# Moving loads, stores and operand work in the feed-forward part of a fused attention kernel

## The chip, the cores and the metric

The kernel runs on one core of one Trainium2 chip. The metric is the device time of one execution in microseconds (us), as the median of several runs. Engines are named as the profile names them: PE (TensorE matmuls), PEld (its weight loads), DVE (VectorE), ACT (ScalarE), POOL (GpSimd), SP (SyncE, whose queue SPq issues nearly all DMAs of this kernel).

## The reference, cut to what matters

Attention over 4 batches, 8 heads, 768 positions and 64 channels, masked to pairs whose keys and queries fall into the same hash bucket (6 sign bits of a projection), and then a feed-forward layer with a piecewise activation on the 3072 tokens:

```python
mask = q_bucket[:, :, :, None] == k_bucket[:, :, None, :]
scores = np.where(mask, scale * np.matmul(q, k.transpose(0, 1, 3, 2)), -1e9)
attn = np.exp(scores - scores.max(-1, keepdims=True))
attn = attn / (attn.sum(-1, keepdims=True) + 1e-09)
x = np.matmul(attn, v).transpose(0, 2, 1, 3).reshape(3072, 512)
h = x @ w_in                                   # 512 x 2048
g = np.where(h >= 1, h, np.where(h <= -1, 0.0, (h + 1) ** 2 / 4))
out = g @ w_out                                # 2048 x 512
```

## The kernel before, in words

Each fp32 factor of a product is split into a high part (rounded to the matmul's input type, fp32r) and a low part (what is left), and a product is three matmuls: high x high, high x low, low x high.

The first part, attention, runs to about 480 us and is not touched. It leaves for each batch b in DRAM the unnormalised output `xd`, the maxima `ed` and the sums' reciprocals `rd`, and the split first weight matrix in SBUF (`wbig` and parts of the tiles `t`) and DRAM (`wq`).

The second part, `ffn`, works on eight chunks of 384 tokens, chunk c = 2b and 2b + 1 of batch b. The order of its work is written out by hand: lists `prep[n]` and `post[n]` hold what is issued before and after the matmuls of step n. `at` appends to the first list, `after` to the second. Each engine, and the DMA queue of SyncE, works in the order in which the program issues.

- **Direct steps**, n = 0 to 31 (480 to 613 us): batch 0. A step is `gemm1` (L772, 12 matmuls into PSUM bank `h`), the activation (ACT: `t`, `z`, L617 and L618; DVE: L623 and L624), the split of the result (`ghi` on ACT, L628; `glo` on DVE, L632), and nine second-layer matmuls (L657, into `y`) of the unit three steps earlier. Beside these DVE splits the blocks of w_out (L70, L74, L78, L82), each from a load into `wraw` (L62, two buffers).
- **Products**, k = 0 to 167 (from 617 us): batches 1 to 3, 56 products each. First-layer blocks of two hidden tiles are computed with seven products instead of eight (`PRODUCTS`, a scheme of Strassen's kind). A product is six matmuls L867, of which the second bank `h` is free only when the product two before it has been read: on ACT by L873 (s = 0) or on DVE by L875 to L887 (s = 1, 3, 4, 5, 6). Then come 4 to 6 matmuls L657. The product's weights are read from a ring of nine tiles (`w_load`, L830), each loaded again from `wc` in DRAM when the product that used it is done.

Three kinds of side work feed the products.

- `w_plan` builds the four summed weight blocks of a pair of hidden tiles: `w_get` loads two blocks from `wq` into `tmp[:, 0]` (L730, L731), `w_sum` adds on DVE into `sumw`, `w_hi` casts on ACT into `tmp[:, 1]` (L739), `w_lo` subtracts on DVE into `tmp[:, 0]`, `w_put` stores both to `wc` (L746, L747).
- `x_plan` builds the fourteen operand tiles of half a batch (cc = 0 or 1): `x_raw` loads four tiles of `xd` into `pc0` to `pc3` (L675); for each of them `x_er` loads a broadcast row of `ed` into `pc4` and of `rd` into `pc5` (L682, two halves each); `x_norm` combines them on DVE (L686, L688); then sums (L697), high parts on ACT (L700) and low parts on DVE (L39).
- `flush` copies a finished `y` on ACT into a tile `ot` (L646, two buffers) and stores it (L647).

Of the kernel before, what the change touches and what calls it, by code (L numbers as in the profile page):

```python
# [22 lines left out]
P = 128  # L23
# [550 lines left out]
def ffn(ctx, tc, wpair, woh, wol, xm, xa, xb, areas, wst, wq, wc, out, prep, post):  # L574
# [29 lines left out]
    def operand(b, o, cc, t):  # L604
        return sets[(b - 1) % 2][cc * 2 * NBLK + 2 * o + t]

# [29 lines left out]
    def flush(c, m):  # L636
# [8 lines left out]
        ot = xp.tile([P, DM], F32, name="ot", bufs=2)  # L645
# [31 lines left out]
    def x_er(b, cc, k):  # L677
        ct, sl = 2 * (k % 2) + cc, slice(k // 2 * CH, (k // 2 + 1) * CH)
        for t, d in ((pc[4], xm.e_d[b]), (pc[5], xm.r_d[b])):
            for h in range(2):  # L680
                r = 2 * ct + h
                nc.sync.dma_start(out=t[64 * h:64 * h + 64], in_=d[r:r + 1, sl].partition_broadcast(64))  # L682

    def x_norm(b, cc, k):
        ct, sv = 2 * (k % 2) + cc, spc[b % 2]
        nc.vector.scalar_tensor_tensor(out=pc[k], in0=pc[4], scalar=sv[:, ct, 0:1], in1=pc[k],  # L686
                                       op0=ALU.mult, op1=ALU.add)
        nc.vector.tensor_tensor(out=pc[k], in0=pc[k], in1=pc[5], op=ALU.mult)  # L688
# [16 lines left out]
    def x_plan(b, cc, raw, norm, made):  # L705

        at(raw, x_raw, b, cc)
        after(raw, x_er, b, cc, 0)
        for k, n in enumerate(norm):
            at(n, x_norm, b, cc, k)  # L710
            if k < 3:
                after(n, x_er, b, cc, k + 1)
        for o, n in made:
# [35 lines left out]
    def w_plan(i, n):  # L749
        at(n, w_get, i)  # L750
        at(n + 1, w_sum, 0)
        at(n + 2, w_sum, 1)
        at(n + 2, w_sum, 2)
        for t in range(2):
            after(n + 2 + t, w_hi, t)
            at(n + 3 + t, w_lo, t)
        at(n + 4, w_put, i)
# [19 lines left out]
    N1 = 2 * NFT  # L777
# [6 lines left out]
    for i in range(NFT // 2):  # L784
        at(8 + i, w_plain, i)
        w_plan(i, (20, 24, 28)[i] if i < 3 else N1 + 6 * (i - 3))
    x_plan(1, 0, 9, (11, 13, 15, 17), ((0, 18), (1, 18), (3, 19), (2, 19), (4, 20), (5, 21), (6, 21)))
    x_plan(1, 1, 22, (24, 25, 26, 27), ((0, 27), (1, 28), (3, 28), (2, 29), (4, 29), (5, 30), (6, 30)))
    for b in (2, 3):
        t0 = N1 + 56 * (b - 2)  # L790
# [4 lines left out]
    at(N1 + 2, lambda: xm.sums_load(*(t[:, 0:NF] for t in pc[4:6]), B - 1))  # L795
    at(N1 + 6, xm.sums_add)
    at(N1 + 6, xm.sums_inv, B - 1)

# [18 lines left out]
    for u in pend:  # L817
# [3 lines left out]
    ring = [t.rearrange("p a b -> p (a b)").bitcast(F32R)[:, n * DM:(n + 1) * DM]  # L821
            for t in [wst.tile([P, DM, 2], I32, name="wraw") for _ in range(2)] for n in range(2)]
    ring += [tu[:, n * DM:(n + 1) * DM] for n in range(3, 6)] + [wpair[15][:, t] for t in range(2)]
    cm, cu = (wst.tile([P, DM], F32, name="wsq")[:, 0:CH] for _ in range(2))
    cv = wst.tile([P, DM], I32, name="wa", bufs=1).bitcast(F32)[:, 0:CH]
    NK = (B - 1) * (NFT // 2) * NBLK

    def w_load(k):
        if k < NK:
            nc.sync.dma_start(out=ring[k % NRING].bitcast(F32),  # L830
# [261 lines left out]
```

## Time and profile before

| | |
|---|---|
| median of the runs | 1049.91 us (1048.38 to 1053.71, 3 runs) |
| the profiled execution | 1052.17 us, span 1050.4 us, mean granted clock 0.993 |
| PE busy | 984.1 us (94%) |
| DVE busy | 793.7 us (76%) |
| ACT busy | 681.1 us (65%) |
| attention, 0 to 500 us | PE 474.1 busy of 500 |
| direct steps, 488.9 to 620.3 us | PE 126.5 busy of 131.4 |
| products 0 to 27, 620.3 to 707.6 us | PE 70.6 busy of 87.3 |
| products 28 to 55, 707.6 to 774.7 us | PE 63.0 busy of 67.1 |
| products 56 to 111, 774.7 to 912.1 us | PE 129.9 busy of 137.4 |
| 49 products, 912.1 to 1022.2 us | PE 110.1 busy of 110.1 |

The stages are cut at ACT's copy L873, which follows every seventh product. Two things are needed to read the numbers. Consecutive matmuls overlap in the records, so a stage is best judged by the time that a product takes in it, not by PE's busy share. And a wait that the profile puts down to DVE or ACT may begin further back: these engines work in order, and one of their own instructions may be waiting for a DMA, which in its turn waited in SyncE's queue.

### The profile page before, as it was taken

Reading aid. Unit: us, or ns where it says so; the run is one execution under the profiler, and the core shown is the slowest. Engines: PE = TensorE matmul, PEld = TensorE weight load, DVE = VectorE, ACT = ScalarE, POOL = GpSimd, SP = SyncE. Lnnn points to the kernel's source line nnn. Section 1 sums busy time; section 2 is a strip of 40 time slices with the busy share of each in tenths; the row PEclk is TensorE's granted clock in tenths of the full one; section 3 lists DMA queues with packets and bytes.
Section 4 is the critical chain, followed back from the end, with each engine's and each line's share of the span. In section 5 each row is a group of like instructions: output and inputs, shape, how many; then the busy total and the mean of one; then the engine's idle time right before and its main releaser. Section 6 shows DMA issues by size and latency. Waiting matters only on the chain.

```text
span 1050.4 us, 15678 instructions
## 1 busy us (share of the span) xinstructions
PE 984.1 (94%) x5036; PEld 893.3 (85%) x5036; DVE 793.7 (76%) x1356; ACT 681.1 (65%) x1489; POOL 344.3 (33%) x412
## 2 busy tenths in 40 slices
PE   5899999999999999999999969879998999999997
PEld 4789989899999999988989858668787888888885
DVE  7779989899999999886789657666765767555553
ACT  5779888899889889886456444344453545454443
POOL 6667767777778778562000000000000000000000
PEclk9999999999999999999999998999999999999999
DMA  3645657776666665643772467847456474454431
GB/s 96 173 119 138 172 152 183 179 185 169 181 168 175 172 170 146 154 109 113 243 232 81 166 218 234 247 158 216 130 148 201 112 198 112 122 169 121 113 88 61
DMA packets 95449, 166.19 MB, mean 158 GB/s; under 512 B 15112, under 2 KB 52616, under 8 KB 95368
## 3 DMA queue, kind: packets, MB, share of 16 engines
q1 hardware_dynamic: 95152, 165.20, 56.3%
q8 instruction: 40, 0.66, 0.3%
q14 instruction: 41, 0.34, 0.1%
q10 hardware_dynamic: 216, 0.00, 0.0%
HBM read 106.13 MB, written 33.87 MB: 133 GB/s over the span
## 4 chain that ended last, share of the span: by engine, by line
PE 60%; DVE 14%; DMA 12%; ACT 8%; issue 3%; SPq 2%; POOL 0%; DVEq 0%; ACTq 0%
PE y L657 14%; PE h L867 11%; PE smax L258 5%; PE s L298 5%; PE o L332 5%; PE o L330 5%; PE o L331 5%; PE s L297 5%; DMA t<-te 5%; PE h L772 3%; DMA pc<-rd 3%; DVE t L623 2%; ACT t L617 2%; ACT z L618 2%; DVE nm L262 2%
## 5 line engine op out<-in xcount | busy, mean ns | idle before, releaser
L306 ACT ACTIVATE ph<-s 128x384 fp32r<-128x384 f32 x380 | 188.1, 495 | 54.0 <-PE s L298 46.2
L262 DVE TENSOR_REDUCE nm<-smax 128x1 f32<-128x768 f32 x186 | 176.5, 949 | 25.9 <-PE smax L258 24.1
L39 POOL TENSOR_TENSOR pl<-pf,ph 128x384 fp32r<-128x384 f32 x128 | 141.2, 1108 | 84.8 <-ACT pf L311 82.7
L623 DVE SCALAR_TENSOR_TENSOR t<-t 128x384 f32<-128x384 f32 x128 | 71.3, 557 | 108.7 <-ACT z L618 108.6
L39 DVE TENSOR_TENSOR pl<-s,ph 128x384 fp32r<-128x384 f32 x256 | 135.9, 545 | 15.7 <-ACT s L311 13.8
L298 PE MATMUL s<-t 128*128 128x384 f32 x384 | 131.5, 343 | 6.3 <-DMA t<-te 6.2
L297 PE MATMUL s<-t 128*128 128x384 f32 x384 | 132.1, 344 | 0.8 <-DVE t L212 0.8
L332 PE MATMUL o<-pl,va 128*128 128x386 f32 x384 | 130.4, 340 | 0.3 <-DVE pl L39 0.3
L330 PE MATMUL o<-ph,va 128*128 128x386 f32 x384 | 130.2, 339 | 0.0
L331 PE MATMUL o<-ph,vb 128*128 128x386 f32 x384 | 129.6, 337 | 0.0
L657 PE MATMUL y<-t,ghi 128*128 128x512 f32 x384 | 125.1, 397 | 0.6 <-ACT ghi L628 0.6
L311 ACT ACTIVATE s<-s 128x384 f32<-128x384 f32 x252 | 125.3, 497 | 0.0
L258 PE MATMUL smax<-t 128*128 128x384 f32 x372 | 100.7, 351 | 5.3 <-DVE nm L262 4.4
L628 ACT CAST ghi<-z 128x384 fp32r<-128x384 f32 x129 | 65.1, 505 | 47.2 <-DVE z L624 42.0
L867 PE MATMUL h<-wbig,t 128*128 128x384 f32 x399 | 83.6, 342 | 6.3 <-DVE wsq L887 4.0
L617 ACT ACTIVATE t<-wsq,mh 128x384 f32<-128x384 f32 x48 | 29.6, 617 | 90.3 <-DVE wsq L881 56.3
L867 PEld LDWEIGHTS h<-wbig,t 128*128 128x128 f32 x399 | 71.6, 190 | 15.5 <-DVE wsq L887 5.2
L657 PEld LDWEIGHTS y<-t,ghi 128*128 128x128 f32 x384 | 71.8, 189 | 12.0 <-ACT ghi L628 1.1
L618 ACT ACTIVATE z<-t,m 128x384 f32<-128x384 f32 x128 | 79.0, 617 | 4.2
L298 PEld LDWEIGHTS s<-t 128*128 128x128 f32 x384 | 72.4, 189 | 10.9 <-DMA t<-te 10.7
L867 PE MATMUL h<-wbig,wraw 128*128 128x384 f32 x321 | 68.2, 347 | 13.9 <-DVE wsq L875 6.7
L258 PEld LDWEIGHTS smax<-t 128*128 128x128 f32 x372 | 64.3, 188 | 19.4 <-DVE nm L262 18.4
(142 smaller groups left out, 2117.5 us busy)
## 6 DMA issues: line engine op xcount, KB each, us to landing
t<-wc SPq DMA_DIRECT2D x92, 256.0 KB
t<-t SPq DMA_DIRECT2D x60, 384.0 KB
wraw<-wc SPq DMA_DIRECT2D x76, 256.0 KB
raw<-in_qk_dram SPq DMA_DIRECT2D x15, 768.0 KB
wraw<-in_w_in_dram SPq DMA_DIRECT2D x16, 512.0 KB
wraw<-in_w_out_dram SPq DMA_DIRECT2D x16, 512.0 KB
wc<-tmp SPq DMA_DIRECT2D x16, 512.0 KB
xd<-xs SPq DMA_DIRECT2D x32, 192.5 KB
```

The lines of the kernel that those rows point to most:

```text
L39: eng.tensor_tensor(out=out, in0=a, in1=b, op=ALU.subtract)
L258: nc.tensor.matmul(out=smax[hd][:, hf, 0:HS], lhsT=t2[:, 0, h, i * P:(i + 1) * P], rhs=t2[:, 1, h, hf * HS:(hf + 1) * HS], start=True, sto ...
L262: nc.vector.tensor_reduce(out=nmp(hd)[:, i:i + 1], in_=smax[hd][:, :, 0:HS], axis=AX.XY, op=ALU.max, negate=True)
L297: nc.tensor.matmul(out=ps[:, 0:HS], lhsT=t1[:, 1, h, ks], rhs=t1[:, 0, h, sl], start=True, stop=False)
L298: nc.tensor.matmul(out=ps[:, 0:HS], lhsT=t2[:, 1, h, ks], rhs=t2[:, 0, h, sl], start=False, stop=True)
L306: nc.scalar.activation(out=ph[:, 0:HS], in_=ps[:, 0:HS], func=AF.Exp, scale=SCALE)
L311: nc.scalar.activation(out=pf, in_=ps[:, 0:HS], func=AF.Exp, scale=SCALE)
L330: nc.tensor.matmul(out=o, lhsT=wa, rhs=ph, start=(jj == 0), stop=False)
L331: nc.tensor.matmul(out=o, lhsT=wb, rhs=ph, start=False, stop=False)
L332: nc.tensor.matmul(out=o, lhsT=wa, rhs=pl, start=False, stop=(jj == NJ - 1))
L657: nc.tensor.matmul(out=ys[c][m], lhsT=g_[:, m * P:(m + 1) * P], rhs=w, start=(first and k == 0), stop=(last and k == 2))
L867: nc.tensor.matmul(out=ps, lhsT=w[:, cs], rhs=x, start=(n == 0 and s not in (2, 3, 6)), stop=(n == 5), skip_group_check=True)
```

## The change

Six edits, all in `ffn` and the list of w_out's splits.

1. `w_lo` writes into `sumw`, over its own input, and `w_put` stores the low half from there; so `tmp[:, 0]` is only read, and the next `w_get` waits for DVE alone. The steps between load, sums, casts and store of a block are given one by one, and the products' blocks stand eight steps apart instead of six.
2. `x_er` issues all sixteen broadcast halves of a half batch at once, each row into a tile of its own (`spread`): tiles that will hold operands later, or parts of `tmp` and `sumw`.
3. The operands are built over more steps: for batches 2 and 3 the norms stay two steps apart, and the seven operands come two steps apart instead of one.
4. `w_load(k + 9)` is issued at the start of product k + 1, behind what is left of product k, and no longer right behind k's matmuls. The ring's first tiles are loaded in direct step 27 and products 0 and 1.
5. `flush` uses, for chunks 2 and later, the two `ot` tiles and two halves of `sumw` in turn; chunks 0 and 1 keep the two `ot` tiles.
6. The splits of w_out's blocks 10 and 11 come one direct step earlier and those from 12 on two steps; the sums of batch 3 move to direct steps 8 and 10.

```diff
+    def spread(b, cc, k, t):
+
+        n = 2 * k + t
+        if b > 1:
+            return sets[(b - 1) % 2][(14, 15, 16, 17, 18, 19, 25, 26)[n]].bitcast(F32)
+        if cc == 1:
+            return cut(ta, n).bitcast(F32)
+        return cut(tflat, n).bitcast(F32) if n < 5 else cut(sflat, n - 5) if n < 7 else pc[5]
...
-        ot = xp.tile([P, DM], F32, name="ot", bufs=2)
+        n = ((c % 2 if c < 2 * B - 2 else 1 - c % 2) * 3 + m) % 4 if c > 1 else 0
+        ot = xp.tile([P, DM], F32, name="ot", bufs=2) if n < 2 else sflat[:, (n - 2) * DM:(n - 1) * DM]
...
-    def x_er(b, cc, k):
-        ct, sl = 2 * (k % 2) + cc, slice(k // 2 * CH, (k // 2 + 1) * CH)
-        for t, d in ((pc[4], xm.e_d[b]), (pc[5], xm.r_d[b])):
-            for h in range(2):
-                r = 2 * ct + h
-                nc.sync.dma_start(out=t[64 * h:64 * h + 64], in_=d[r:r + 1, sl].partition_broadcast(64))
+    def x_er(b, cc):
+        for k in range(4):
+            ct, sl = 2 * (k % 2) + cc, slice(k // 2 * CH, (k // 2 + 1) * CH)
+            for t, d in enumerate((xm.e_d[b], xm.r_d[b])):
+                for h in range(2):
+                    r = 2 * ct + h
+                    nc.sync.dma_start(out=spread(b, cc, k, t)[64 * h:64 * h + 64],
+                                      in_=d[r:r + 1, sl].partition_broadcast(64))
...
-        sub(nc, nc.vector, raw_w[:, sl], sum_w[:, sl], hi_w[:, sl].bitcast(F32))
+        sub(nc, nc.vector, sum_w[:, sl].bitcast(F32R), sum_w[:, sl], hi_w[:, sl].bitcast(F32))
...
-        nc.sync.dma_start(out=wc[i][:, 3:7, 1], in_=raw_w.bitcast(F32))
+        nc.sync.dma_start(out=wc[i][:, 3:7, 1], in_=sum_w)
...
-        w_plan(i, (20, 24, 28)[i] if i < 3 else N1 + 6 * (i - 3))
-    x_plan(1, 0, 9, (11, 13, 15, 17), ((0, 18), (1, 18), (3, 19), (2, 19), (4, 20), (5, 21), (6, 21)))
-    x_plan(1, 1, 22, (24, 25, 26, 27), ((0, 27), (1, 28), (3, 28), (2, 29), (4, 29), (5, 30), (6, 30)))
+    for i in range(3):
+        n = 17 + 4 * i
+        w_plan(i, n, n + 2, n + 3, (n + 3, n + 3), (n + 4, n + 4), n + 5)
+    w_plan(3, 29, 31, N1 + 1, (N1 + 1, N1 + 2), (N1 + 2, N1 + 3), N1 + 5)
+    for i in range(4, NFT // 2):
+        n = N1 + 8 * i - 28
+        w_plan(i, n, n + 4, n + 5, (n + 5, n + 6), (n + 6, n + 7), n + 9)
...
+    x_plan(1, 0, 11, 11, (13, 14, 15, 16), (17, 17, 18, 18, 19, 19, 20))
+    x_plan(1, 1, 22, 24, (26, 26, 27, 27), (28, 28, 29, 29, 30, 30, 31))
     for b in (2, 3):
...
-            t = t0 + (14, 35)[cc] - (8 if b == 3 else 0)
-            x_plan(b, cc, t, [t + 2 + 2 * k for k in range(4)],
-                   [(o, t + 10 + k) for k, o in enumerate((0, 1, 3, 2, 4, 5, 6))])
+            t = N1 + 56 * (b - 2) + (3, 30)[cc]
+            x_plan(b, cc, t, t, [t + 4 + 2 * k for k in range(4)], [t + 12 + 2 * k for k in range(7)])
+
+    at(27, ring_staged)
+    for k in range(4, NRING):
+        at(N1 + (k > 6), w_load, k)
...
+        if k > 0:
+            w_load(k - 1 + NRING)
         for fn, a in prep.pop(N1 + k, ()):
             fn(*a)
...
-        w_load(k + NRING)
...
+            need -= (i > 9) + (i > 11)
```

SyncE's queue in the changed kernel, from the end of the first train of rows (it began with product 3's step; ahead of the first row below stand `xsva`, four `xd` tiles and twelve more row halves) to the stores of chunk 1. `wraw<-wc` and `t_1_75<-wc` are ring loads, `tmp<-wq` the block loads, `wc<-` their stores.

```order
L695 DMA t_1_75<-ed_69 64x384 x2
L695 DMA t_1_75<-rd_107 64x384 x2
L777 DMA wraw<-wc_98 128x512
L742 DMA tmp<-wq_89 128x2x256
L743 DMA tmp<-wq_90 128x512
L659 DMA out_dram<-ot 128x512
L777 DMA t_1_75<-wc_98 128x512
L758 DMA wc_100<-tmp 128x4x256
L759 DMA wc_100<-sumw 128x4x256
L659 DMA out_dram<-ot 128x512 x2
```

The same stores before, in products 2 to 5:

```order
L830 DMA wraw<-wc_98 128x512 x2
L746 DMA wc_100<-tmp 128x4x256
L747 DMA wc_100<-tmp 128x4x256
L830 DMA t_1_75<-wc_98 128x512
L647 DMA out_dram<-ot 128x512
L830 DMA t_1_75<-wc_99 128x512
L647 DMA out_dram<-ot 128x512 x2
L730 DMA tmp<-wq_89 128x2x256
L731 DMA tmp<-wq_90 128x512
```

Before, no row of batch 2 stands ahead of chunk 1's stores (its first stands eleven products later); now the whole train does, and the block's load stands ahead of the previous block's store.

SyncE's queue in the changed kernel where chunks 2 and 3 are stored, products 58 and 59. The two `wbig` rows stand four times each in turn; they are shown once.

```order
L659 DMA out_dram<-ot 128x512
L777 DMA t_1_75<-wc_98 128x512
L684 DMA xsvb<-xd_62 128x4x2
L687 DMA pc_6071<-xd_62 128x384
L687 DMA pc_6072<-xd_62 128x384
L687 DMA pc_6073<-xd_62 128x384
L687 DMA pc_6074<-xd_62 128x384
L695 DMA wbig<-ed_70 64x384 x2
L695 DMA wbig<-rd_108 64x384 x2
L659 DMA out_dram<-ot 128x512
```

Before, all six stores of these chunks (L647) stood ahead of `xsvb<-xd_62`; now five of them stand behind the train.

VectorE in products 7 and 8 of the changed kernel (L634 and L635 are the old L623 and L624, L643 the old L632, L899 the old L875, L911 the old L887; L700 and L702 the norms):

```order
L911 TENSOR_TENSOR wsq<-h_6065,wsq 128x384
L643 TENSOR_TENSOR glo<-z,ghi 128x384
L634 SCALAR_TENSOR_TENSOR t<-t 128x384
L635 TENSOR_TENSOR z<-t,z 128x384
L700 SCALAR_TENSOR_TENSOR pc_6071<-t_2_79,xsva,pc_6071 128x384
L702 TENSOR_TENSOR pc_6071<-pc_6071,t_2_79 128x384
L643 TENSOR_TENSOR glo<-z,ghi 128x384
L39 TENSOR_TENSOR sumw<-tmp 128x512
L899 TENSOR_TENSOR wsq<-h_6065,wsq 128x384
```

The norm of batch 2's first tile stands here nine products earlier than before, and the sum into `sumw` stands ahead of the add that frees product 8's bank.

More of the change, by code (lines that the diff above doesn't have):

```diff
@@ L703, in x_lo, with x_plan @@
         sub(nc, nc.vector, operand(b, o, cc, 1), pc[HOME[o]], operand(b, o, cc, 0).bitcast(F32))
-    def x_plan(b, cc, raw, norm, made):
+    def x_plan(b, cc, raw, er, norm, made):
         at(raw, x_raw, b, cc)
-        after(raw, x_er, b, cc, 0)
+        at(er, x_er, b, cc)
         for k, n in enumerate(norm):
             at(n, x_norm, b, cc, k)
-            if k < 3:
-                after(n, x_er, b, cc, k + 1)
-        for o, n in made:
+        for o, n in zip((0, 1, 3, 2, 4, 5, 6), made):
             if o in SUMS:
```

52 lines of the change are left out of this document (27 added, 25 removed).

## The prediction

> **What bounds the kernel now.** I read first the busy times by stretch, cut where the stages change (columns: span, busy us and instructions of PE, PEld, DVE, ACT, POOL, granted clock, DMA share, GB/s): direct steps, products 0-27, 28-55, 56-111, and a stretch of 49 products with no operand work.
>
> ```profile
> 488.90:620.30 131.40, 126.47 (x621) 113.09 (x622) 104.56 (x197) 72.13 (x139) 0.00 (x0) 0.99 0.54 174
> 620.30:707.60 87.30, 70.60 (x321) 59.18 (x319) 56.08 (x112) 36.81 (x71) 0.00 (x0) 0.96 0.67 212
> 707.60:774.70 67.10, 63.01 (x303) 54.18 (x304) 47.41 (x94) 32.71 (x63) 0.00 (x0) 1.00 0.55 162
> 774.70:912.10 137.40, 129.94 (x626) 113.20 (x625) 89.33 (x175) 65.61 (x125) 0.00 (x0) 0.99 0.54 154
> 912.10:1022.20 110.10, 110.10 (x548) 98.90 (x547) 61.37 (x120) 52.83 (x99) 0.00 (x0) 1.00 0.44 127
> ```
>
> In the last row TensorE never pauses: 110.1 / 49 = 2.247 us a product, 62.9 for 28. The rows above lose 87.3 - 62.9 = 24.4, 67.1 - 62.9 = 4.2 and 137.4 - 125.8 = 11.6 us. Then the timeline: TensorE's large waits, and the rows of VectorE in which they begin.
>
> ```profile
> 600.53 2.36 PE L772 MATMUL h<-t,t 128*128 128x384 f32 x12 [1.76 <-ACT t L617]
> 611.09 0.69 DVE L39 TENSOR_TENSOR sumw<-tmp 128x512 f32<-128x512 f32 x1 [5.24 <-DMA tmp<-wq]
> 614.77 0.50 PE L657 MATMUL y<-woh,glo 128*128 128x512 f32 x1 [3.06 <-DVE glo L632]
> 629.13 0.69 DVE L39 TENSOR_TENSOR sumw<-tmp 128x512 f32<-128x512 f32 x1 [6.55 <-DMA tmp<-wq]
> 630.35 2.29 PE L867 MATMUL h<-wbig,wraw 128*128 128x384 f32 x6 [5.50 <-DVE wsq L875]
> 636.98 1.23 PE L867 MATMUL h<-wbig,t 128*128 128x384 f32 x6
> 797.57 0.62 DVE L686 SCALAR_TENSOR_TENSOR pc<-pc,xsvb,pc 128x384 f32<-128x384 f32 x1 [5.83 <-DMA pc<-ed]
> 799.78 1.27 PE L867 MATMUL h<-t,wraw 128*128 128x384 f32 x3 [5.07 <-DVE wsq L875]
> ```
>
> TensorE is named as waiting for VectorE, but VectorE, which works in order, was itself waiting for a weight block or a broadcast row that SyncE had issued late. Before product 0 TensorE loses 1.76 + 3.06 and some 0.7 of slow matmuls. The six-matmul group after the 5.50 wait takes 2.29 instead of 1.23: a long pause is paid twice. In all 24.4 + 4.2 + 11.6 + 5.5 = 45.7 us. Without any of it the profiled execution's 1052.17 would be 1006.5. That is the floor; the question is what takes the place of these waits.
>
> **What it removes.** L730's wait for the store of the block before goes, since the low half no longer lands in its buffer, and the block is used two to four steps after its load instead of one. The rows e and r get sixteen homes, so none waits for L686 and L688 any more. Every DMA wait in the fence above loses its cause: taken at the whole 45.7, before what follows.
>
> **What it adds on SyncE's queue.** All sixteen rows and four raw tiles now go out in one train. Issue prices (start, us; the last line is from the list of DMA issues, KB each):
>
> ```profile
> 440.51 0.59 SPq L539 DMA_DIRECT2D t<-rd  x1
> ...
> 444.35 0.59 SPq L539 DMA_DIRECT2D t<-rd  x1
> ...
> 600.02 0.33 SPq L647 DMA_DIRECT2D out_dram<-ot  x1
> ...
> 606.55 0.56 SPq L730 DMA_DIRECT2D tmp<-wq  x1
> ...
> 639.07 0.38 SPq L830 DMA_DIRECT2D t<-wc  x1
> ...
> 657.35 0.53 SPq L672 DMA_DIRECT2D xsva<-xd  x1
> 657.92 2.03 SPq L675 DMA_DIRECT2D pc<-xd  x4
> ...
> 585.19 1.09 SPq L682 DMA_DIRECT2D pc<-ed  x2
> ...
> pc<-ed SPq DMA_DIRECT2D x48, 96.0 KB
> ```
>
> Six row issues lie between 440.51 and 444.35: 0.64 each, at most; the pair at 585.19 gives 0.55. I take 0.62: a train is 0.53 + 2.03 + 16 x 0.62 = 12.5 us, 5.6 products. Weight loads stand nine products (20 us) ahead, so they survive it. Output stores do not stand ahead, and ScalarE needs their tiles back:
>
> ```profile
> 592.81 1.06 ACT L646 COPY ot<-y 128x512 f32<-128x512 f32 x2
> 596.46 1.06 SPq L647 DMA_DIRECT2D out_dram<-ot  x2
> 599.41 0.58 ACT L646 COPY ot<-y 128x512 f32<-128x512 f32 x1 [5.53 <-DMA out_dram<-ot]
> ```
>
> ScalarE's third copy waits until the first store has landed, 2.95 us after that issue began; here it stood 5.53 and TensorE lost the 1.76 above. Chunk 1 still has only two tiles (`n = 0` for c < 2), and its first store now stands behind the train of product 3 and one weight block. The chain of waits has TensorE's pace:
>
> ```profile
> 926.56 1.17 PE y L657 x5
> 927.73 1.05 PE h L867 x6
> ```
>
> Count from the start of product 0: a product with five y matmuls takes 2.20, products 3-5 with four 1.98, the seventh of a block with six 2.45. The train starts when product 2's matmuls end, 5.9, and ends at 18.4; a load 0.4, two block loads 1.2, store at 20.0, landed about 22.9. The third copy is due at 12.6. Queued behind it on ScalarE are the cast ghi of product 4, both activations of product 6 and the copy of product 7. TensorE wants that ghi in the fourth y matmul of product 7, at 15.0 + 1.05 + 0.7 = 16.7, and gets it at 22.9 + 0.6 + 0.5 = 24.0: **7 us**.
>
> The same happens with chunks 2 and 3: the second store stands behind the train of product 59, and the sixth copy reuses its tile.
>
> ```profile
> 779.06 0.59 ACT L646 COPY ot<-y 128x512 f32<-128x512 f32 x1
> 787.04 1.15 ACT L646 COPY ot<-y 128x512 f32<-128x512 f32 x2
> ```
>
> Product 56 starts near 773.6, so the first copy is at 5.5 and the sixth at 14.0 after it. Train from 6.4 to 18.9, store landed at 21.9, ghi of product 60 at 23.0, wanted in the fourth y matmul of product 63, at 15.7 + 1.05 + 0.7 = 17.4: **5.5 us**. Bounds for each: 0 (ScalarE's later work turns out to be early enough) and the 10 and 8 us for which the copy itself is late.
>
> The block load behind the first train lands late too, and the sum into `sumw` must now wait for the store out of `sumw`.
>
> ```profile
> 580.92 2.95 DMA wc<-tmp
> 660.00:680.00 20.00, 17.20 (x81) 14.04 (x79) 13.44 (x27) 8.13 (x15) 0.00 (x0) 1.00 0.90 267
> ```
>
> At share 0.90 the DMA engines moved 267 GB/s, so some 297 at most. From 18.4 on some 2.8 MB stand up to that store (rows in flight 0.5, two weight loads and an output tile 0.8, two block loads 0.5, both halves 1.0): 9.5 us, plus about 1: 29. VectorE, freed at 24.0, gets there near 28. I take **2 us** (0 to 4; 6 if ScalarE did not stall first). [...]
>
> **Operand work.** VectorE in products 33 to 35:
>
> ```profile
> 717.73 0.55 DVE L884 TENSOR_TENSOR wa<-wa,h 128x384 f32<-128x384 f32 x1
> 719.62 0.56 DVE L623 SCALAR_TENSOR_TENSOR t<-t 128x384 f32<-128x384 f32 x1 [1.33 <-ACT z L618]
> 720.21 0.56 DVE L624 TENSOR_TENSOR z<-t,z 128x384 f32<-128x384 f32 x1
> 720.68 0.55 DVE L887 TENSOR_TENSOR wsq<-h,wsq 128x384 f32<-128x384 f32 x1
> 721.15 0.55 DVE L632 TENSOR_TENSOR glo<-z,ghi 128x384 fp32r<-128x384 f32 x1
> 722.57 0.56 DVE L623 SCALAR_TENSOR_TENSOR t<-t 128x384 f32<-128x384 f32 x1 [0.87 <-ACT z L618]
> ```
>
> From start to start an operation costs 0.47, a pair L623/L624 1.06. Seven products hold 5 adds, 4 low halves and 4 such pairs, 8.5 us, and three holes (1.42 after L884, 0.95 after L887's low half, one like it after L881) that no operand work fills, since it is queued ahead of the add and not between add and pair: 11.8 of 15.7, spare 3.9. A half batch of operands costs 4 x 1.12 + 11 x 0.47 = 9.7, a weight block 2.7. Products 9-28 hold about 16 us of such work against 19.5 / 7 x 3.9 = 10.9: short by 5, less what the banks absorb: **4 us** (1 to 8). Products 28-55 hold 12.4 against 15.6, later ones less: **1 us** for pieces that fall together.
>
> **Direct steps.** There the train of step 11 stands ahead of the w_out load that L70 of step 14 needs.
>
> ```profile
> 523.59 0.74 DVE L78 SCALAR_TENSOR_TENSOR wa<-wraw,wsc,wa 128x512 int32<-128x512 int32 x1
> 536.78 0.42 DVE L70 TENSOR_SCALAR wa<-wraw 128x512 int32<-128x512 int32 x1
> 560.00:580.00 20.00, 20.00 (x102) 18.18 (x101) 19.65 (x39) 13.24 (x26) 0.00 (x0) 1.00 0.31 97
> ```
>
> SyncE first waits for L78 (524.3), then issues three copies (some 2 us), then the train: 527 to 539, load landed about 542, wanted at 538-539 (L70 comes one step later than at 536.78, less what is ahead of it). VectorE is 3-4 us late and, full from there (19.65 of 20), loses more. A lag like that cost 3.06 at 614.77: **3 us** (0 to 6). For half-clock matmuls after the two long stalls **2 us** (0 to 5).
>
> **Sum:** 3 + 7 + 2 + 4 + 1 + 5.5 + 2 = 24.5 comes back of 45.7; 1052.17 - 21.2 = 1031. The median shown is 2.3 below the profiled execution: **1028 us**.
>
> **Rivals.** *The trains hold nothing up* (chance 0.21). ScalarE has slack, or issues overlap, and both store terms with their clock go: 14.5 us less, 1014. For it: ScalarE is busy under half the time; against it: the 599.41 row, where the third copy waited just so. [...]
>
> *VectorE is the bound* (0.13). Its lag from step 14 never heals, deficits are 12 instead of 5 and the direct steps lose 6: 11 more, 1039.
>
> *The change does little* (0.05). The late loads were the transfers' own time, and each comes as late from its new place: only the blocks' wait for their own store (some 3 us) goes: 1047.
>
> *Slower* (0.05): the ring runs dry. If in a train each issue waits for the landing of the one eight before, and a landing takes 12 us instead of 3, a train lasts 30 us. It decides from 20 us, the lead of the weight loads; beyond it each train stops TensorE for 10 us or more, and four trains in the products (3, 30, 59, 86) make some 1028 + 45 = 1073. Against it: 660-680 moved 267 GB/s, more than a train asks (2.4 MB in 12.5 us, 190 GB/s).
>
> **Numbers.** Forecast 1028, chance 0.56, own range 1020 to 1036. With the rivals 1009 to 1043 leaves out under two in ten. About 0.5% (5.2 us) is what a measurement here tells from no change: faster 0.90, same 0.05, slower 0.05.
>
> **What would show it.** Right: no VectorE wait for DMA over 2 us outside product 8; ScalarE's L658 waiting 8-10 us for its store near products 5 and 61, TensorE waiting for ghi just after; products 28-55 in 63-65 us. Wrong: those copies start without a wait (then 1014), VectorE still waits for wq or rd rows, or TensorE waits for a ring load.

## The result, and the profile after

The changed kernel takes 1033.97 us (median of four runs, 1031.63 to 1037.66) against 1050.39 for the kernel before in the same comparison: a ratio of 0.9844, 95% interval 0.9804 to 0.9883. The forecast was 1028, own range 1020 to 1036, so the time lies inside the range and 2 us from its upper end. The profiled execution took 1037.66 us with a span of 1035.9; the one of before took 1052.17. So 14.5 us went between the two traces where the sum expected 21.2.

Where they went is read from one row of ScalarE. Its copy in the first product of every block of seven (L897, L873 before) marks the pace. The timeline of ScalarE, changed kernel (start, duration in us), products 0, 7, 28, 56, 63 and 112:

```profile
620.48 0.47 ACT L897 COPY wsq<-h 128x384 f32<-128x384 f32 x1
...
646.87 0.47 ACT L897 COPY wsq<-h 128x384 f32<-128x384 f32 x1
...
699.98 0.47 ACT L897 COPY wsq<-h 128x384 f32<-128x384 f32 x1
...
764.34 0.47 ACT L897 COPY wsq<-h 128x384 f32<-128x384 f32 x1
...
787.83 0.47 ACT L897 COPY wsq<-h 128x384 f32<-128x384 f32 x1
...
899.93 0.47 ACT L897 COPY wsq<-h 128x384 f32<-128x384 f32 x1
```

From copy to copy is a stage. "Direct" runs from the first matmul of the direct steps (483.12 here, 480.85 before) to product 0's copy; "no loss" is 2.247 us a product, from the prediction's stretch without pauses. All in us; the kernels of the experiments are read in the same way, one trace each. The copy follows ScalarE and not TensorE: in the changed kernel the matmuls of product 7 began at 633.95 and its copy came at 646.87, so a stall in product 7 counts in "0-6". Shifts of about 1 us between neighbouring stages say nothing (14.8 lies under "no loss").

| kernel | direct | 0-6 | 7-27 | 28-55 | 56-62 | 63-111 | median |
|---|---|---|---|---|---|---|---|
| no loss | | 15.7 | 47.2 | 62.9 | 15.7 | 110.1 | |
| before | 139.5 | 24.8 | 62.5 | 67.1 | 15.7 | 121.7 | 1050 |
| changed | 137.4 | 26.4 | 53.1 | 64.4 | 23.5 | 112.1 | 1034.0 |
| e1_actq | 137.5 | 18.1 | 60.7 | 64.3 | 17.4 | 110.4 | 1024.6 |
| e2_merge | 180.9 | 47.6 | 52.9 | 84.0 | 45.4 | 132.9 | 1162.3 |
| e3_weights | 145.8 | 32.9 | 64.4 | 62.4 | 23.1 | 112.4 | 1059.4 |
| e4_rows | 131.0 | 17.5 | 55.3 | 67.3 | 15.7 | 121.0 | 1026.2 |
| e5_stagger | 137.7 | 19.7 | 53.0 | 64.4 | 16.1 | 112.1 | 1018.0 |
| e6_w12 | 135.3 | 26.4 | 53.1 | 64.4 | 23.1 | 112.2 | 1031.9 |
| e7_pool | 136.8 | 26.5 | 54.5 | 64.6 | 22.8 | 113.6 | 1035.4 |
| e8_actq_sum | 138.2 | 17.5 | 60.0 | 64.3 | 17.3 | 110.4 | 1024.0 |
| e11_t5 | 138.1 | 16.7 | 57.1 | 64.3 | 14.8 | 113.1 | 1022.0 |
| e9_direct | 133.7 | 19.4 | 52.9 | 64.4 | 15.5 | 112.2 | 1015.5 |
| e10_later | 134.9 | 16.7 | 56.9 | 64.4 | 14.8 | 112.5 | 1016.6 |
| e12_need | 134.3 | 26.7 | 53.5 | 64.3 | 24.1 | 112.0 | 1033.1 |

The change won 9.4 us in products 7 to 27, 2.7 in 28 to 55, 9.6 in 63 to 111 and 2.1 in the direct steps, and gave back 1.6 in products 0 to 6 and 7.8 in 56 to 62. Attention, which it does not touch, ended 2.3 us later in this execution. As much was won after product 111, and 1.4 of it behind the last matmul (6.9 us from its start to the end before, 5.5 now). There ScalarE's copy of a `y` waited, before, until one of only two tiles was stored; with edit 5's four tiles it waits for no store. ScalarE before:

```profile
1046.04 0.58 ACT L646 COPY ot<-y 128x512 f32<-128x512 f32 x1 [1.51 <-DMA out_dram<-ot]
```

The busy times of the changed kernel by stretch, to be held against the first fence of the prediction:

```profile
491.10:620.50 129.40, 125.06 (x618) 111.00 (x619) 106.54 (x202) 72.26 (x140) 0.00 (x0) 1.00 0.57 185
620.50:700.00 79.50, 68.35 (x323) 59.64 (x322) 53.78 (x107) 36.89 (x72) 0.00 (x0) 0.94 0.70 217
700.00:764.30 64.30, 63.07 (x311) 55.51 (x310) 47.13 (x93) 32.30 (x62) 0.00 (x0) 1.00 0.56 173
764.30:899.90 135.60, 127.72 (x626) 114.23 (x625) 89.23 (x175) 65.53 (x125) 0.00 (x0) 0.97 0.54 156
```

In the second row TensorE pauses for 11 us, as in the fourth for 8. TensorE's waits after the attention, from 490 to 910 us, are now few; these are all of 0.5 us or more, but for three of 1.0 to 1.1 that end on VectorE:

```profile
491.09 2.36 PE L801 MATMUL h<-t,wbig 128*128 128x384 f32 x12 [1.57 <-ACT t L628]
548.90 2.35 PE L801 MATMUL h<-t,wbig 128*128 128x384 f32 x12 [2.92 <-ACT t L628]
645.46 1.22 PE L669 MATMUL y<-t,ghi 128*128 128x512 f32 x2 [9.57 <-ACT ghi L639]
786.41 1.22 PE L669 MATMUL y<-t,ghi 128*128 128x512 f32 x2 [7.88 <-ACT ghi L639]
```

The two long ones wait for ghi, a cast on ScalarE. What ScalarE itself waited for just ahead of them, and what SyncE was doing (L687 loads of raw tiles, L695 of rows, L742/L743 of block 4, L659 the output store):

```profile
644.41 0.58 ACT L658 COPY ot<-y 128x512 f32<-128x512 f32 x1 [10.36 <-DMA out_dram<-ot]
...
785.37 0.58 ACT L658 COPY ot<-y 128x512 f32<-128x512 f32 x1 [9.06 <-DMA out_dram<-ot]
```

```profile
624.93 0.53 SPq L684 DMA_DIRECT2D xsva<-xd  x1
625.57 1.99 SPq L687 DMA_DIRECT2D pc<-xd  x4
627.61 1.12 SPq L695 DMA_DIRECT2D t<-ed  x2
...
636.92 1.23 SPq L695 DMA_DIRECT2D t<-rd  x2
638.25 0.52 SPq L777 DMA_DIRECT2D wraw<-wc  x1
638.88 0.55 SPq L742 DMA_DIRECT2D tmp<-wq  x1
639.48 0.59 SPq L743 DMA_DIRECT2D tmp<-wq  x1
640.16 0.38 SPq L659 DMA_DIRECT2D out_dram<-ot  x1
```

The store stands behind a train of 13.2 us (624.93 to 638.15): ScalarE stands until it has landed, and TensorE stands because ScalarE does.

### The profile page after: what moved, and what is told of

Same layout as the page of the kernel before. It is cut to its first block, busy times and chain, and to the rows that moved or that the text cites. A ratio compares the mean times of both kernels' runs of the same rounds, so it can differ in the third digit from the quotient of the medians.

```text
span 1035.9 us, 15651 instructions
## 1 busy us (share of the span) xinstructions
PE 979.7 (95%) x5036; PEld 895.1 (86%) x5036; DVE 793.9 (77%) x1356; ACT 680.9 (66%) x1489; POOL 343.5 (33%) x412
## 4 chain that ended last, share of the span: by engine, by line
PE 66%; DVE 10%; DMA 8%; ACT 7%; SPq 5%; issue 2%; POOL 1%; ACTq 0%; DVEq 0%
PE y L669 19%; PE h L892 14%; PE smax L258 5%; PE s L298 5%; PE o L332 5%; PE o L330 5%; PE o L331 5%; PE s L297 4%; DMA t<-te 4%; PE h L801 4%; SPq L695 3%; DVE nm L262 2%; DMA wraw<-in_w_in_dram 1%; DVE t L634 1%; ACT t L628 1%
## 5 line engine op out<-in xcount | busy, mean ns | idle before, releaser
L306 ACT ACTIVATE ph<-s 128x384 fp32r<-128x384 f32 x380 | 188.0, 495 | 55.3 <-PE s L298 47.8
L634 DVE SCALAR_TENSOR_TENSOR t<-t 128x384 f32<-128x384 f32 x128 | 71.4, 557 | 107.2 <-ACT z L629 107.0
L39 DVE TENSOR_TENSOR pl<-s,ph 128x384 fp32r<-128x384 f32 x256 | 135.8, 545 | 14.7 <-ACT s L311 11.0
L669 PE MATMUL y<-t,ghi 128*128 128x512 f32 x384 | 126.5, 401 | 17.5 <-ACT ghi L639 17.4
L669 PEld LDWEIGHTS y<-t,ghi 128*128 128x128 f32 x384 | 72.3, 191 | 29.3 <-ACT ghi L639 18.8
L643 DVE TENSOR_TENSOR glo<-z,ghi 128x384 fp32r<-128x384 f32 x128 | 70.4, 550 | 19.3 <-ACT ghi L639 19.3
L892 PEld LDWEIGHTS h<-wbig,t 128*128 128x128 f32 x399 | 72.3, 190 | 6.6 <-DVE wsq L911 1.4
```

The lines of the kernel that those rows point to most:

```text
L39: eng.tensor_tensor(out=out, in0=a, in1=b, op=ALU.subtract)
L306: nc.scalar.activation(out=ph[:, 0:HS], in_=ps[:, 0:HS], func=AF.Exp, scale=SCALE)
L669: nc.tensor.matmul(out=ys[c][m], lhsT=g_[:, m * P:(m + 1) * P], rhs=w, start=(first and k == 0), stop=(last and k == 2))
L892: nc.tensor.matmul(out=ps, lhsT=w[:, cs], rhs=x, start=(n == 0 and s not in (2, 3, 6)), stop=(n == 5), skip_group_check=True)
```

## The experiments

Each kernel is the changed one with the edit shown; all were timed against the kernel before, and their ratios carry 95% intervals.

### e1_actq: the stores leave the queue of the train

```
-        nc.sync.dma_start(out=out[r0:r0 + P, :], in_=ot)
+        (nc.scalar if c in (1, 2, 3) else nc.sync).dma_start(out=out[r0:r0 + P, :], in_=ot)
```

> The changed kernel with one edit: the output stores of chunks 1, 2 and 3 are issued by ScalarE right behind the copy that fills the tile, no longer by SyncE behind its trains. Theory (stores behind trains): ScalarE's waits of 10.36 and 9.06 us for its own stores go, and with them TensorE's 9.57 and 7.88 us and some 2 us of slow matmuls behind them. Products 0-6 take 16 to 17 us (26.4 now), products 56-62 16 us (23.5 now); the time falls from 1034 to about 1015. Rival (VectorE is the bound there anyway): the gain comes back as VectorE waits, products 7-27 grow from 53.1 to 58 us or more, and the time stays above 1022. Rival (ScalarE pays for the issues): TensorE waits for ScalarE in other places near the nine stores, 3 to 5 us in all.

Measured: 1024.64, ratio 0.9766 (0.9742 to 0.979). Both waits of ScalarE are gone and both stages fall, to 18.1 and 17.4. But products 7 to 27 grow to 60.7, and the first rival's numbers hold as well. What came in place of the stall, from the timelines of VectorE and TensorE:

```profile
643.86 0.69 DVE L39 TENSOR_TENSOR sumw<-tmp 128x512 f32<-128x512 f32 x1 [7.57 <-DMA wc<-sumw]
```

```profile
645.07 2.29 PE L892 MATMUL h<-wbig,wraw 128*128 128x384 f32 x6 [7.49 <-DVE wsq L899]
```

So the cause of the stall is shown (the store behind the train), and the gain was half of what its size promised. It is not VectorE's amount of work that took it, as the rival had it: VectorE stood. It waited for the store of block 3 out of `sumw`, which was issued at 636.75, behind the same train (620.50 to 633.77), and had been covered by ScalarE's stall.

### e8_actq_sum: the covered wait moved

```
-        w_plan(i, n, n + 4, n + 5, (n + 5, n + 6), (n + 6, n + 7), n + 9)
+        m = n + 3 if i == 4 else n
+        w_plan(i, n, m + 4, m + 5, (m + 5, m + 6), (m + 6, m + 7), m + 9)
```

This stands on top of e1's edit.

> The kernel with ScalarE's own store issues (e1), and weight block 4 summed and stored three products later. In e1 VectorE stood 7.57 us at product 8 for the store of the block before, out of sumw. Theory (this wait is only late by its place behind the train): the wait falls under 2 us, products 7-27 go from 60.7 to 53 to 55, the time from 1024.6 to about 1017. Rival (the work is short there anyway): VectorE's wait goes, but products 14-34 get longer by as much, 1022 or more.

Measured: 1024.04, ratio 0.9758 (0.9731 to 0.9785); no difference from e1. The store of block 3 still landed when it did, and VectorE waited 4.16 us for it. It then waited a second time, for the store of block 4, which now comes three products later:

```profile
643.38 0.69 DVE L39 TENSOR_TENSOR sumw<-tmp 128x512 f32<-128x512 f32 x1 [4.16 <-DMA wc<-sumw]
...
661.31 0.69 DVE L39 TENSOR_TENSOR sumw<-tmp 128x512 f32<-128x512 f32 x1 [2.73 <-DMA wc<-sumw]
```

TensorE's one wait of 7.49 became four of 1.0 to 2.1 between 645 and 665 us. The forecast was wrong in the wait (under 2 us) and in the time (1017). The rival's time is met, its reason only in part: products 14 to 34 grew from 51.6 in e1 to 54.4, but VectorE's wait did not go. The work that moved with the reader of the late store found no free room here.

### e5_stagger: the train cut in four

```
+            for k in range(4):
+                at(er + 2 * k, x_er, b, cc, (k,))
```

The pieces go out at the start and two, four and six products later, for the batches of the products only; as many loads into the same homes.

> The changed kernel with the trains of the products cut in four: each piece of rows (four loads) goes out four products before its norm instead of all sixteen at once, into the same homes. The trains of the direct steps stay. Theory (length of the train, not the number of loads or the homes, is what costs): chunk 1's and chunk 2's first stores stand behind 5 us of issues instead of 13; TensorE's waits of 9.57 and 7.88 us fall under 2; products 0-6 take 17 to 19 us, 7-27 53 to 57, 56-62 16 to 17; the time is about 1016. Rival (the rows' bytes crowd the other transfers wherever they go): waits for stores over 5 us remain, 1026 or more. Rival (the old spacing of rows in e4 was right, homes bring nothing): products 14-27 and 63-111 as slow as there (40.7 and 121 us).

Measured: 1017.98, ratio 0.9697 (0.9674 to 0.9721). The theory holds within 2 us. Products 56 to 62 take 16.1; in 0 to 6 (19.7, over the 17 to 19 expected) some of the wait is left, since the raw tiles and the first piece still stand ahead of the first store:

```profile
633.23 0.58 ACT L658 COPY ot<-y 128x512 f32<-128x512 f32 x1 [3.34 <-DMA out_dram<-ot]
```

Products 7 to 27 stay at 53.0: with the long train gone the store of block 3 is issued at 629 and VectorE has no wait of 1 us for a DMA there. One cause, the long train ahead of both stores, stood behind both waits. The rows' bytes are not it, as they are the same.

### e11_t5: the train whole, but two products later

```
-            t = N1 + 56 * (b - 2) + (3, 30)[cc]
+            t = N1 + 56 * (b - 2) + (5, 30)[cc]
```

> The changed kernel with one number changed: the first half of a batch's operands starts at product 5 of the 56 instead of 3, the train still in one piece. SyncE then issues the first output store, the load of block 4 and both stores of block 3 before the train. Theory (it is the order on SyncE's queue, not the number of issues): the store waits of 10.36 and 9.06 us go with the train as long as it was (13 us); products 0-6 take 17 to 18 us (26.4), 7-27 about 53, 56-62 about 16.5 (23.5); the time is 1016 to 1018, as with the train cut in four (1018). Rival (a train of 13 us always stands ahead of something that is due): a wait of 5 us or more appears elsewhere, at a ring load or at the later stores, and the time stays over 1024.

Measured: 1021.96, ratio 0.9735 (0.9717 to 0.9752), 4 us over what the theory said. ScalarE's waits for its stores in the products are gone with the train still 14.7 us long (629.68 to 644.41) (products 0 to 6 in 16.7, 56 to 62 in 14.8), so order alone removes them. The 4 us are in products 7 to 27 (57.1, about 53 expected). The rival is right in kind, below its size of 5 us and 1024: a train of this length found something else that was due, here a weight block of the ring. Timeline of TensorE:

```profile
650.22 2.04 PE L892 MATMUL h<-wbig,t 128*128 128x384 f32 x6 [3.35 <-DMA t<-wc]
...
784.65 1.29 PE L892 MATMUL h<-t,t 128*128 128x384 f32 x6 [1.88 <-DMA t<-wc]
```

### e2_merge: half the issues

```
-                for h in range(2):
-                    r = 2 * ct + h
-                    nc.sync.dma_start(out=spread(b, cc, k, t)[64 * h:64 * h + 64],
-                                      in_=d[r:r + 1, sl].partition_broadcast(64))
+                nc.sync.dma_start(out=spread(b, cc, k, t),
+                                  in_=d[2 * ct:2 * ct + 2, sl].unsqueeze(1).broadcast_to([2, 64, CH]))
```

> The changed kernel with each pair of broadcast row loads (two rows of 64 partitions) written as one DMA of 128 partitions: eight issues in a train instead of sixteen, the same bytes. Theory A (an issue has a price of its own): a train falls from 13.2 us to about 8, ScalarE's store waits from 10.4 and 9.1 to about 5 and 4, TensorE loses 10 us less: about 1024. Theory B (an issue is paid by its bytes or rows): one issue takes 1.2 us, the train stays at 13, the time at 1034.

Measured: 1162.27, ratio 1.1077 (1.1049 to 1.1106); neither theory. SyncE's rows, and the stretch 672 to 692:

```profile
668.10 0.54 SPq L693 DMA_DIRECT2D t<-ed  x1
668.68 0.52 SPq L693 DMA_DIRECT2D t<-rd  x1
...
671.41 3.82 SPq L693 DMA_DIRECT2D wbig<-rd  x1
675.27 3.82 SPq L693 DMA_DIRECT2D wbig<-ed  x1
```

```profile
672.00:692.00 20.00, 4.39 (x22) 3.63 (x20) 2.36 (x5) 1.71 (x3) 0.00 (x0) 0.70 0.13 50
```

The first two issues cost 0.53 each for 192 KB, as much as one of 96 KB before (0.56): so far theory A. The third takes 2.12 and the rest 3.4 to 4.7, three of them 3.82; the DMA engines then move 50 GB/s at a share of 0.13, as much as two of sixteen engines at work would show (16 x 0.13 = 2.1). The merged load has an outermost dimension of two; that this is the reason was not shown. The rows' part of the train grew to 23 us (668.10 to 691.15). What such a train does was the prediction's fourth rival, and it can be read here: ScalarE waits 31 us for a store, twice, and TensorE twice for the ring. Most is lost in the direct steps (180.9 us), where ScalarE waits 33.34 for w_out.

```profile
801.07 2.26 PE L890 MATMUL h<-wbig,wraw 128*128 128x384 f32 x6 [14.82 <-DMA wraw<-wc]
...
979.93 1.30 PE L890 MATMUL h<-t,t 128*128 128x384 f32 x3 [12.73 <-DMA t<-wc]
```

### e3_weights and e4_rows: one half of the change at a time

e3 takes the weight blocks back, e4 the rows, the operand plan and the place of batch 3's sums:

```
e3:
-        sub(nc, nc.vector, sum_w[:, sl].bitcast(F32R), sum_w[:, sl], hi_w[:, sl].bitcast(F32))
+        sub(nc, nc.vector, raw_w[:, sl], sum_w[:, sl], hi_w[:, sl].bitcast(F32))
...
-        w_plan(i, n, n + 4, n + 5, (n + 5, n + 6), (n + 6, n + 7), n + 9)
+        n = (20, 24, 28)[i] if i < 3 else N1 + 6 * (i - 3)
+        w_plan(i, n, n + 1, n + 2, (n + 2, n + 3), (n + 3, n + 4), n + 4)
e4:
-                    nc.sync.dma_start(out=spread(b, cc, k, t)[64 * h:64 * h + 64],
+        for t, d in ((pc[4], xm.e_d[b]), (pc[5], xm.r_d[b])):
...
-            x_plan(b, cc, t, t, [t + 4 + 2 * k for k in range(4)], [t + 12 + 2 * k for k in range(7)])
+            x_plan(b, cc, t, [t + 2 + 2 * k for k in range(4)],
+                   [(o, t + 10 + k) for k, o in enumerate((0, 1, 3, 2, 4, 5, 6))])
```

> The changed kernel with the weight blocks as in the kernel before: low half back into the buffer of the load, one product from load to first use. The rows keep their homes. Theory (the blocks' late loads were a part of the loss): VectorE waits for wq again, 5 us or more in the direct steps and 5 to 8 us near product 7, since the load now also stands behind the train of product 3; the time is 1040 to 1050. Rival (the rows made all of the gain): 1034, within 3 us.

> The changed kernel with the rows e and r back in two shared tiles and the operand work at its old products (the sums of the last batch's rows are also back at products 2 and 6). The weight blocks stay as changed. Theory: without trains no copy waits for its store, so products 0-6 take about 17 us and 56-62 about 16; in exchange VectorE waits again for rows (2 to 6 us near products 9, 33 and 60) and has its work in clumps. The two about cancel: 1025 to 1035. Rival (the homes are the main gain): 1042 or more. Rival (the homes cost more than they bring): 1022 or less.

Measured: e3 1059.42, ratio 1.0088 (1.0059 to 1.0117); e4 1026.18, ratio 0.9778 (0.9753 to 0.9802). With trains but without the early loads the kernel is slower than before, and slower than the forecast of e3 allowed (1040 to 1050): it has the store stall and the waits for wq one after the other.

```profile
615.93 0.69 DVE L39 TENSOR_TENSOR sumw<-tmp 128x512 f32<-128x512 f32 x1 [7.68 <-DMA tmp<-wq]
...
634.24 0.69 DVE L39 TENSOR_TENSOR sumw<-tmp 128x512 f32<-128x512 f32 x1 [5.87 <-DMA tmp<-wq]
```

With the weights alone it is 7.8 us faster than with the whole change, within e4's 1025 to 1035. What the rows' part (homes, trains, operand plan and those sums together) costs and brings is in the table, changed against e4: 6.4 us lost in the direct steps, 8.9 in products 0 to 6 and 7.8 in 56 to 62; 2.2, 2.9 and 8.9 won in 7-27, 28-55 and 63-111, where e4 still has its work in clumps and its waits for rows:

```profile
772.49 0.62 DVE L698 SCALAR_TENSOR_TENSOR pc<-pc,xsvb,pc 128x384 f32<-128x384 f32 x1 [5.18 <-DMA pc<-rd]
```

Edit 4 (the place of the ring's loads) and edit 5 were not taken back alone; no run here shows what they are worth by themselves. The 1.4 us behind the last matmul, put down to edit 5 above, is read from the two traces alone.

### e6_w12, e12_need and e9_direct: the direct steps

e6 moves the train of step 11 to step 12, behind one w_out load; e12 takes back the last piece of the change; e9 has e5's pieces and cuts this train too, with the norms of its half one step later:

```
e6:
-    x_plan(1, 0, 11, 11, (13, 14, 15, 16), (17, 17, 18, 18, 19, 19, 20))
+    x_plan(1, 0, 11, 12, (13, 14, 15, 16), (17, 17, 18, 18, 19, 19, 20))
e12:
-            need -= (i > 9) + (i > 11)
e9 (with e5):
+            at(er + 2 * k if b > 1 else norm[k] - 2, x_er, b, cc, (k,))
...
-    x_plan(1, 0, 11, 11, (13, 14, 15, 16), (17, 17, 18, 18, 19, 19, 20))
+    x_plan(1, 0, 11, 11, (14, 15, 16, 17), (17, 17, 18, 18, 19, 19, 20))
```

> The changed kernel with one edit: the rows' train of the direct steps goes out at step 12 instead of 11, so behind the w_out load of block 12 and three copies of weight blocks. Theory (that load, 10.5 us late, made the direct steps lose): ScalarE's and VectorE's waits for w_out at step 14 fall under 3 us, TensorE's 2.92 us wait and the slow matmuls behind it go; the stretch from the first direct step to product 0 takes 131 to 134 us (137.4 now; 131.0 with the old rows), the time is 1028 to 1031. Rival (the rows then come too late for their norms): VectorE waits for ed or rd rows 3 us or more, no gain.

> The changed kernel without the last piece of the change, the earlier conversion of the late w_out blocks (blocks 10 and 11 one step later again, 12 and up two steps). The train of step 11 stays. Theory (the train only hurts because the earlier conversion wants its load right behind it): the wait for w_out at step 14 (VectorE 7 us, TensorE 2.92) goes, since the block is wanted two steps later; but conversion, weight sums and operands fall closer together in steps 24 to 31, where TensorE waited 3.06 us for a low half before, and that wait or a like one returns; the stretch from the first direct step to product 0 takes 135 to 138 us (137.4), the time is 1031 to 1036. Rival (the earlier conversion alone made the direct steps faster): 140 us or more, 1037 or more. Rival (it was of no use): 131 to 134 us, 1028 or less.

> The kernel with the trains of the products cut in four (e5), and the train of the direct steps cut too: a piece two steps before its norm, the norms of the first half one step later; the w_out load of block 12 then stands behind no row. Theory: no wait for w_out at step 14 and none over 1.5 us for rows; the stretch from the first direct step to product 0 takes 131 to 133 us (137.7 in e5, 135.3 in e6), the time is 1011 to 1014 (1018 in e5). Rival (something else in the direct steps, for instance the second half's train at step 24, costs the rest): 135 us or more, 1015 to 1018.

Measured: e6 1031.88 (ratio 0.983, 0.9799 to 0.9862), e12 1033.06 (0.9827, 0.9788 to 0.9865), e9 1015.52 (0.9674, 0.9659 to 0.9688). In the changed kernel ScalarE stands at step 14 for w_out; in e6 it does not, but VectorE then waits for rows:

```profile
547.70 0.68 ACT L69 ACTIVATE wsq<-wraw 128x512 f32<-128x512 f32 x1 [10.54 <-DMA wraw<-in_w_out_dram]
```

```profile
535.74 0.67 ACT L69 ACTIVATE wsq<-wraw 128x512 f32<-128x512 f32 x1 [1.40 <-DMA wraw<-in_w_out_dram]
```

```profile
538.29 0.62 DVE L700 SCALAR_TENSOR_TENSOR pc<-tmp,xsvb,pc 128x384 f32<-128x384 f32 x1 [5.14 <-DMA tmp<-ed]
```

So e6 shows both its theory and its rival: TensorE's 2.92 us wait is gone, but the stage, at 135.3, stays above the 131 to 134 expected, and the median is not clear of the changed kernel's (the two intervals overlap). In e12 the w_out wait that was to go is still there on ScalarE (and VectorE waits 6.32), while TensorE's 2.92 is gone:

```profile
543.99 0.68 ACT L69 ACTIVATE wsq<-wraw 128x512 f32<-128x512 f32 x1 [7.65 <-DMA wraw<-in_w_out_dram]
```

Its stage took 134.3, between the ranges of its theory and of the rival that the earlier conversion is of no use; it is 3.1 under the changed kernel, in a single trace, and the medians do not differ. What that piece is worth without a train ahead of it stays open. e9 has neither a wait for w_out over 2.2 us nor one for rows of 1 us there, and is with e10 the fastest kernel of the study, 1.8% under the changed one (1015.52 / 1033.97). But its stage, at 133.7, is above its theory's 131 to 133, and its time, 1.5 over what the theory said, lies in the rival's 1015 to 1018: what else the direct steps lose against e4's 131.0 stays open.

### e10_later: e9 and e11 together

The edits are those of e9 and e11.

> The last kernel with the start of the first half at product 5 instead of 3 as well. Theory: the 2.55 us that TensorE still waits for ghi in e5 near product 7 go, and block 4's sums fall no longer together with the norms: products 0-6 take 17 to 18 us (19.7 in e5), 7-13 16 to 18 (18.9), 56-62 16; the time is 1007 to 1011. Rival (work only moves into products 14-34): these grow by 2 us or more (51.5 in e5), 1011 to 1014.

Measured: 1016.55, ratio 0.9681 (0.9656 to 0.9707), no difference from e9. Products 0 to 6 give 2.7 us, and 7 to 27 take 4.0 (14 to 34 take 53.5, 51.5 in e9): the rival.

### e7_pool: low halves on GpSimd

```
-        sub(nc, nc.vector, operand(b, o, cc, 1), pc[HOME[o]], operand(b, o, cc, 0).bitcast(F32))
+        sub(nc, nc.gpsimd if b > 1 else nc.vector, operand(b, o, cc, 1), pc[HOME[o]], operand(b, o, cc, 0).bitcast(F32))
```

> The changed kernel with the low halves of the operands of batches 2 and 3 computed on GpSimd, which is idle there, instead of VectorE: 28 operations of 0.47 us less on VectorE. Theory (VectorE is short by some 5 us in products 9-28): products 14-34 take 48 to 49 us (51.5 now, 47.2 without loss), the rest stays: about 1031. Rival (it is not VectorE's sum but the order of its work): the products 14-34 stay at 51 us. Rival (GpSimd slows VectorE): VectorE's operations get longer, 0.56 to 0.6 us or more, and the time rises.

Measured: 1035.36, ratio 0.9866 (0.9839 to 0.9892): no gain, and products 7 to 27 grew by 1.4. The groups of VectorE's operations from 640 to 1009 us, of the changed kernel and then of e7 (count, busy us, mean ns):

```profile
L635 DVE TENSOR_TENSOR z<-t,z 128x384 f32<-128x384 f32 x88 | 49.1, 558 | 3.0
L899 DVE TENSOR_TENSOR wsq<-h,wsq 128x384 f32<-128x384 f32 x22 | 12.1, 551 | 0.0
```

```profile
L635 DVE TENSOR_TENSOR z<-t,z 128x384 f32<-128x384 f32 x89 | 61.3, 688 | 3.1
...
L899 DVE TENSOR_TENSOR wsq<-h,wsq 128x384 f32<-128x384 f32 x23 | 12.6, 549 | 0.0
```

and single operations of it:

```profile
734.84 1.29 DVE L635 TENSOR_TENSOR z<-t,z 128x384 f32<-128x384 f32 x1
...
739.88 1.28 DVE L635 TENSOR_TENSOR z<-t,z 128x384 f32<-128x384 f32 x1
```

The 28 operations that went saved VectorE some 13 us (28 x 0.47), and L635 alone gave 12.2 back (61.3 - 49.1). What the operations show is the rival that GpSimd slows VectorE: some of L635's additions take 1.28 to 1.29 us instead of 0.56. The median is not clear of the changed kernel's.

## Why the prediction was right or wrong

**Right in kind, and in the likeliest case.** Of its four signs of being right three are in the trace: ScalarE's third and sixth copies stand 10.36 and 9.06 us for a store (8 to 10 expected), TensorE waits for ghi just behind, products 28 to 55 take 64.4 us (63 to 65). None of its signs of being wrong is there: VectorE waits 0.81 us at most for a row and never for wq, and TensorE never for the ring. The fourth sign failed: VectorE was to have no wait for a DMA over 2 us outside product 8, and it has two in the direct steps.

```profile
547.71 0.43 DVE L70 TENSOR_SCALAR wa<-wraw 128x512 int32<-128x512 int32 x1 [6.81 <-DMA wraw<-in_w_out_dram]
...
603.26 0.69 DVE L39 TENSOR_TENSOR sumw<-tmp 128x512 f32<-128x512 f32 x1 [4.27 <-DMA wc<-sumw]
```

The first belongs to the term for the direct steps. The second is a price of edit 1, the sum that waits for the store out of `sumw`; the prediction looked for it in product 8 alone. TensorE has no wait of 0.5 us between 580 and 635, so it cost nothing that shows.

The rival that the trains hold nothing up (1014) falls with ScalarE's waits of 10.36 and 9.06 us: they end with stores that stood behind 13.2 and 13.0 us of issues in one queue (769.24 to 782.25 the second). The rival that VectorE's lag never heals (1039) falls with the direct stage, and the one that little happens (1047) with the time.

**By size the sum was 6 to 7 us short.** Term by term, us:

| term | predicted | measured |
|---|---|---|
| direct steps, left over | 3 | 6.4 over e4 |
| store wait of chunk 1 | 7 | 9.57 |
| put, get and VectorE in 7-27 | 2 + 4 | 4 |
| products 28-55 | 1 | 1.4 |
| store wait of chunk 2 | 5.5 | 7.88 |
| half-clock matmuls | 2 | 4 |

The right column adds up to 33.3, 8.8 over the left; the floor was 2.9 too high (see the direct steps), which leaves 5.9.

The last row is read behind the two stalls of TensorE's timeline:

```profile
645.46 1.22 PE L669 MATMUL y<-t,ghi 128*128 128x512 f32 x2 [9.57 <-ACT ghi L639]
646.47 2.12 PE L892 MATMUL h<-wbig,t 128*128 128x384 f32 x6
...
650.37 1.22 PE L892 MATMUL h<-wbig,wraw 128*128 128x384 f32 x6
```

Seven y and six h matmuls between 645.46 and 650.37 take 4.9 us where the prediction's pace gives 7 x 0.235 + 1.05 = 2.7; the same thirteen behind 786.41 take 4.5. That is 2.2 and 1.8 us; the granted clock was 0.52 and 0.58 in these two stretches. What products 7 to 27 lose beside it is 5.9 less some 1.9 of the first (the rest of it falls before the copy that ends products 0 to 6).

*Chunk 1.* The train began where it was put, 6.0 us after product 0 (618.89; 5.9 predicted), and ended at 19.3 instead of 18.4, mostly because a row took 0.66 from start to start and not 0.62 (sixteen between 627.61 and 638.15); the store was issued at 21.3 (20.0) and let ScalarE go 4.25 us later, where the one row taken as a measure had 2.95. The DMA share was 1.02 (323 GB/s) in those 4.25 us and 0.69 (243 GB/s) in the 2.95. The mis-sized part is the landing, and the train's pace.

*Chunk 2.* All of SyncE's times were met within 0.5 us; TensorE came to the missing ghi 15.4 us after product 56 began, not 17.4. The count of y matmuls was off by one product there.

*Direct steps.* The w_out load was named as the cause, and it is the cause of TensorE's 2.92 (gone in e6 and e9). But the train took 13.8 us there (528.78 to 542.58), and the load issued behind it landed 5.0 later; VectorE was 6.81 late instead of 3 to 4, and ScalarE, which the term leaves out, stood 10.54. The term itself came from one quoted wait of 3.06 us, while TensorE waited in two places (2.92 here, 1.0 for a low half later). The 6.4 holds more than the train, since e4 also has batch 3's sums outside these steps. The floor was off as well: e4 does the stage in 131.0, 8.4 under the kernel before, where adding up waits gave 5.5. The two errors cancel, which is luck: the stage was to get 2.5 us faster and got 2.1. It is luck too that the 1.76 us at 600.53 went: ScalarE's copy, whose wait for its store had caused it, still waits 5.26 us (603.97), but TensorE no longer loses by it.

*Put and get.* The 2 us came as 0 in the changed kernel, and as 7.49 in e1, where the prediction had 6 for the case that ScalarE did not stall first. It also named the time: the store was to land 29 us after product 0, and in e1 it landed at 29.4 (643.86, with product 0 at 614.46). The prediction's "297 at most" is no ceiling, though: from 545 to 555 the changed kernel moved 357 GB/s at a share of 1.02.

*VectorE in products 9 to 28.* The size fits (4 here; 5.8 and 5.7 in e5 and e9, which have no long stall), but that the sum of its work is the reason was not isolated: e7 was to do it and met something else. For it speaks that the loss of products 0 to 27 stays when its pieces are moved: 9.4 us in e9, 10.6 in e10 (72.3 and 73.5 against 62.9).

**What was not seen.** The prediction treated the rows' part as a gain with a cost. By e4 it is a net loss of 7.8 us as written, and a gain of 10.7 when its trains are cut (e9 against e4). Homes and the wider operand plan were worth having together; no run here separates the two. Issuing all rows at once, which homes permit but do not ask for, was not worth it. Nor has the sum a term for the 1.4 us that went behind the last matmul with edit 5's tiles.

## What to carry to other kernels

A transfer that gets a home of its own no longer waits for the readers of a shared tile, and so can be issued early (VectorE's wait for a row was 5.83 us before and 0.81 at most in the changed kernel). Issue it in pieces still: here what stood behind it on the queue paid for its whole length (ScalarE waited 10.36 us for the store behind the whole train, 3.34 in e5 with the train cut in four). The first to pay here were stores, which nobody had placed ahead of time. Look at which buffer comes back through a late store, which engine asks for it next, and what that engine has queued behind the question. When a stall is removed, look for a second wait with the same cause that the first had covered: remove the cause (here the long train ahead of both stores, by cutting it or by placing it later), not the one wait.

## What the runs showed of the hardware that was not expected

A load that broadcasts two rows to 128 partitions, written as one DMA, moved 50 GB/s at a DMA share of 0.13, where the loads of 64 partitions went out at one of 96 KB every 0.66 us, some 149 GB/s: fewer issues were far slower.

With 28 operations on GpSimd instead of VectorE (the seven from 664 to 698 us in e7 took 1.01 to 1.26 us each) VectorE's L635 took 688 ns in the mean instead of 558, and 1.28 to 1.29 us in single rows, while additions with one operand in PSUM (L899) kept their 550 ns (551 and 549). Why L635 got longer was not shown. The idle engine was no free place for this work: the time stayed where it was (1035.36 us against 1033.97).
